# Linear-recurrence attention with a mixture of experts on one core: state products in four column tiles, squares kept in the keys' tile, the bounded norm's last two VectorE operations folded into one, and one state product given to ScalarE

## The chip, the core and the metric

The kernel runs on one core of a Trainium2 chip. The metric is the device time of one execution in microseconds, the median of several runs. The kernel before takes 1791.55 us (median of 3 runs, 1791.02 to 1792.45).

## What is computed

The reference has two parts. The first is a linear recurrence with complex decay, per batch (4) and head (8), over 768 steps with head dimension 48:

```python
mag = np.sqrt(a_re * a_re + a_im * a_im)
scale = np.minimum(mag, 0.999) / (mag + 1e-06)
a_re_n, a_im_n = (a_re * scale, a_im * scale)
for t in range(S):
    new_re = ar * S_re - ai * S_im          # ar, ai: step t's decay
    new_im = ar * S_im + ai * S_re
    kv = np.einsum('bhd,bhe->bhde', k[:, :, t], v[:, :, t])
    S_re, S_im = (new_re + kv, new_im)
    y[:, :, t] = np.einsum('bhd,bhde->bhe', q[:, :, t], S_re)
```

The second takes the outputs as 3072 tokens of 384 channels through 8 experts, `relu(x @ w1[e]) @ w2[e]` with 1024 hidden channels, weighted by a matrix that eight rounds of row and column normalisation make from `exp(x @ w_gate - max)`.

## The kernel before, in words

**Tokens and units.** The 3072 tokens are cut into 12 units of 256 steps (three for each batch entry), a unit into two chunks of 128 steps. Phase 1 (`phase1`, 0 to about 600 us) does the attention of unit i and at the same time experts 0 and 1 for unit i-1. Phases 2a and 2b do the normalisation and the experts 2 to 7, and touch nothing that the change touches.

**Elementwise part, `elem(i)` and `chain`.** For each unit VectorE and ScalarE turn the decays `z` into bounded decays (lines 386 to 400), form the running products of the decays over the chunk (`scan`, `cmul`, lines 283 to 288), and from their squared magnitude (lines 409 to 417) make keys divided by the running product (`kh`, line 420) and queries multiplied by it (written over `z`, line 422). In the bounded norm, line 396 gives `zz` as a Square on ScalarE, line 397 gives `x = min(-0.4995*y0, 1)` on VectorE, and line 398 gives `x = (zz + 0.75) * x` on VectorE. The first unit, `elem(0, scratch=True)`, goes in two halves with tiles of its own; units 1 to 11 go whole, on 128 x 768 elements a plane.

**Chunks, `mix(i)`.** For each chunk, 12 transfers (line 441) bring keys and queries into `ks` and `qs` (six `ks<-kh`, six `qs<-z`), with 112 used partitions: real parts in 0 to 47, imaginary parts in 64 to 111. TensorE transposes the keys (`keys`, line 460), multiplies keys with queries (`scores`, line 474), keys with values (`state`, line 469: the new state contribution `U`, 112 x 48 for each of 8 heads), and masked scores and old state with values and queries (`outs`, line 491). `outs` runs in four column tiles of the array, 32 columns each, one head in each tile. All these operands are four-byte floats; each such matmul is two instructions in the trace. VectorE then makes the next state: `tm = S0 + U` (line 517, left out where the state starts at zero), `sa = tm * rr` (line 524), two half products into `sb` (lines 526 and 527), and `S1 = sa + sb` (line 528). The last chunk of a batch entry makes no state, so 20 of the 24 chunks do this.

**Order.** TensorE's order is written out by hand: for unit i, 16 pieces of expert work of unit i-1 are sent, each of an `l2` (lines 158 to 160) and a first-layer product `ph` (lines 179 to 181); after piece n, from n = LEAD on (11 for unit 1, 10, 8, 6, then 4), one step of `mix` follows: keys, then scores and state, then nothing, then outs and the next chunk's keys. ScalarE copies each `ph` out twice (`hh`, `hf`, lines 185 and 186), VectorE subtracts them (`hl`, line 187). `ph` has two buffers. The orders of VectorE, ScalarE and the DMA queue of SyncE in this phase come from a scheduler that simulates the program, so an edit in one place can move instructions in others.

**Names.** `U` is a PSUM tile; `tm` and `sa` have one buffer each; `sq` (the squares of lines 390 and 409) has a tile of its own, `kh` another.

Of the kernel before, what the change touches and what calls it, by code (L numbers as in the profile page):

```python
# [6 lines left out]
F32 = mybir.dt.float32  # L7
F32R = mybir.dt.float32r
U8 = mybir.dt.uint8
AF = mybir.ActivationFunctionType  # L10
ALU = mybir.AluOpType
AX = mybir.AxisListType

H, D = 8, 48
# [8 lines left out]
SK = 112  # L23
# [20 lines left out]
def slot(h):  # L44
    return (h % 4) * 128 + (h // 4) * 80
# [9 lines left out]
class Net:  # L55
# [9 lines left out]
    def build(self):  # L65
        tc, nc = self.tc, self.nc
        DR = bass.MemoryType.DRAM
        PS = bass.MemoryType.PSUM
        with ExitStack() as ctx:
            dram = ctx.enter_context(tc.tile_pool(name="dram", bufs=1, space=DR))  # L70
            cst = ctx.enter_context(tc.tile_pool(name="cst", bufs=1))
            self.wp = ctx.enter_context(tc.tile_pool(name="wp", bufs=RING))
            self.psA = ctx.enter_context(tc.tile_pool(name="psA", bufs=2, space=PS))

            self.ones = cst.tile([128, 128], F32, name="ones")
            nc.vector.memset(self.ones, 1.0)
            warm = cst.tile([128, 1], F32, name="warm")
            nc.scalar.activation(warm, self.ones[:, 0:1], AF.Abs_reciprocal_sqrt)
            self.ident = cst.tile([128, 128], F32, name="ident")
            nc.sync.dma_start(self.ident, self.idn)  # L80
            self.nident = cst.tile([128, 128], F32R, name="nident")
            nc.scalar.activation(self.nident, self.ident, AF.Copy, scale=-1.0)
            self.mask = cst.tile([128, 4, CH], U8, name="mask")
            tri = cst.tile([128, CH], F32, name="tri")
            nc.sync.dma_start(tri, self.msk)
            for j in range(4):
                nc.vector.tensor_copy(self.mask[:, j, :], tri)
            self.bm05 = cst.tile([128, 1], F32, name="bm05")
            nc.vector.memset(self.bm05, -0.5)
            self.wgs = cst.tile([128, NCT, 2 * E], F32R, name="wgs")  # L90
            self.two = cst.tile([2 * E, E], F32, name="two")
            nc.vector.tensor_tensor(self.two, self.ident[:2 * E, :E], self.ident[:2 * E, E:2 * E], ALU.add)
            wgr = cst.tile([128, NCT, E], F32, name="wgr")
            nc.sync.dma_start(wgr, self.wg)
            nc.scalar.activation(self.wgs[:, :, :E], wgr, AF.Copy)
            nc.vector.tensor_tensor(self.wgs[:, :, E:], wgr, self.wgs[:, :, :E].bitcast(F32), ALU.subtract)
            self.P = cst.tile([128, self.ntt, E], F32, name="P")

            ns = self.N // SUB
            self.fl = cst.tile([128, ns * (NCT * NCH + 2) + 2], F32, name="fl")  # L100
            self.ok = cst.tile([128, 9], F32, name="ok")
            self.oki = cst.tile([1, 1], mybir.dt.int32, name="oki")
            self.wt = {}
            self.x_d = [dram.tile([128, NS, 2, NCT, 2, CH], F32, name=f"x_d{u}") for u in range(self.N // UN)]
            self.ye_d = [[dram.tile([128, C], F32, name=f"ye_d{u}_{i}") for i in range(self.ntt)] for u in range(2)]
            self.dram = dram

            with ExitStack() as c2, tc.manual_schedule(engines={mybir.EngineType.PE}):
                with ExitStack() as c1:
                    with ExitStack() as ca:  # L110
                        self.phase1(c1, ca)
                    self.phase2a(c2)
                self.phase2b(c2)
            flag = nc.values_load(self.oki[0:1, 0:1], min_val=0, max_val=1)
            with tc.If(flag < 1):
                with ExitStack() as c3:
                    self.general(c3)
# [257 lines left out]
    def chain(self, i, ns_, zt, qk, alloc):  # L375
        nc = self.nc
        V = nc.vector
        full = ns_.stop - ns_.start == NCH
        n0 = ns_.start
        G = NCT * (ns_.stop - n0)  # L380

        def cut(t):
            return t if full else t.rearrange("p a (c n) t -> p a c n t", n=NCH)[:, :, :, n0, :]

        z, qk = cut(zt[:, :, :, :CH]), cut(qk)
        fl, ns = self.fl, self.N // SUB
        base = 2 * ns + ns * NCT * NCH
        f0, f1 = (i, ns + i) if n0 == 0 else (base, base + 1)
        sq, x, y0, zz = alloc("sq"), alloc("x"), alloc("y0"), alloc("zz")
        nc.scalar.activation(sq, z, AF.Square, accum_out=fl[:, f0:f0 + 1])  # L390
        V.scalar_tensor_tensor(x, sq[:, 0], 1e-20, sq[:, 1], ALU.max, ALU.add)
        nc.scalar.activation(y0, x, AF.Abs_reciprocal_sqrt)
        nc.scalar.activation(zz, y0, AF.Square, accum_out=fl[:, f1:f1 + 1])
        V.tensor_tensor(x, x, zz, ALU.mult)
        V.scalar_tensor_tensor(y0, x, -3.0, y0, ALU.add, ALU.mult)
        nc.scalar.activation(zz, y0, AF.Square, bias=self.bm05, scale=-0.5e-6)
        V.tensor_scalar(x, y0, -0.4995, 1.0, ALU.mult, ALU.min)
        V.scalar_tensor_tensor(x, zz, 0.75, x, ALU.add, ALU.mult)
        for a in range(2):
            V.tensor_tensor(z[:, a], z[:, a], x, ALU.mult)  # L400
        if full or n0 == 0:
            self.scan(z, alloc)
        else:
            with self.tc.issue_after(self.last.ins):
                self.scan(z, alloc)
        for j in range(CH, ZW):
            nc.scalar.activation(cut(zt[:, :, :, j:j + 1]), z[:, :, :, CH - 1:CH], AF.Copy)
        sq, x, g0 = alloc("sq"), alloc("x"), alloc("g0")
        nc.scalar.activation(sq, z, AF.Square)
        V.scalar_tensor_tensor(x, sq[:, 0], 1e-26, sq[:, 1], ALU.max, ALU.add)  # L410
        o = 2 * ns + i * NCT * NCH + n0 * NCT
        nc.scalar.activation(fl[:, o:o + G], x[:, :, CH - 1], AF.Copy)
        nc.scalar.activation(g0, x, AF.Abs_reciprocal_sqrt)
        act = nc.scalar.activation(g0, g0, AF.Square)
        V.tensor_tensor(x, x, g0, ALU.mult)
        self.gl = V.scalar_tensor_tensor(g0, x, -2.0, g0, ALU.add, ALU.mult)
        V.scalar_tensor_tensor(x, g0, -1.0, qk[:, 1], ALU.mult, ALU.mult)
        kh = alloc("kh")
        for a in range(2):
            V.tensor_tensor(kh[:, a], x, z[:, a], ALU.mult)  # L420
        for a in range(2):
            dve = V.tensor_tensor(z[:, a], z[:, a], qk[:, 0], ALU.mult)
        if i == 0:
            self.acts.append(act)
            self.act0, self.dve0 = act, dve

    def mix(self, i):
        nc, tmp = self.nc, self.tmp
        vt = self.vt[i]
# [4 lines left out]
        for c in range(NCH):  # L434
# [29 lines left out]
            def state(g, c=c, U=U, kts=kts, lastc=lastc):  # L464
                if lastc:
                    return
                for j in range(4):
                    h = 4 * g + j
                    nc.tensor.matmul(U[:, h, :], kts[g][:, j, :], vt[:, c, slot(h):slot(h) + D], start=True, stop=True)  # L469

            def scores(g, i=i, c=c, ks=ks, qs=qs, sss=sss):
                sp = self.psS.tile([128, 4, CH], F32, tag="s", name=f"sp{i}_{c}_{g}")
# [37 lines left out]
            if not lastc:  # L510
                sh = [SK, 2, H // 2, D]
                Uv = U.rearrange("p (b q) d -> p b q d", b=2)
                if first:
                    tm = Uv
                else:
                    tm = tmp.tile([SK, H, D], F32, tag="tm", name=f"tm{i}_{c}", bufs=1).rearrange("p (b q) d -> p b q d", b=2)
                    nc.vector.tensor_tensor(tm, heads(S0), Uv, ALU.add)
                sa = tmp.tile([SK, H, D], F32, tag="sa", name=f"sa{i}_{c}", bufs=1).rearrange("p (b q) d -> p b q d", b=2)

                def bc(t):  # L520
                    return t.rearrange("p (b q) -> p b q", b=2).unsqueeze(3).broadcast_to([t.shape[0], 2, H // 2, D])

                sbv = self.sb.rearrange("p (b q) d -> p b q d", b=2)
                nc.vector.tensor_tensor(sa, tm, bc(rr), ALU.mult)
                h0, h1 = slice(0, D), slice(64, 64 + D)
                nc.vector.tensor_tensor(sbv[h0], tm[h1], bc(R[h1]), ALU.mult)
                nc.vector.tensor_tensor(sbv[h1], tm[h0], bc(rn[h0]), ALU.mult)
                nc.vector.tensor_tensor(heads(S1), sa, sbv, ALU.add)
                self.ist = 1 - self.ist
# [617 lines left out]
```

## Time and profile before

| what | value |
|---|---|
| median of 3 runs | 1791.55 us |
| the profiled execution's own time | 1792.06 us |
| its span, first to last instruction | 1790.3 us |
| mean granted TensorE clock | 0.994 |
| busy: TensorE matmuls, VectorE, ScalarE | 98%, 76%, 41% of the span |
| phase 1 (attention, experts 0 and 1) | 0 to about 600 us |

Times in the rows are microseconds; starts count from the first instruction of the profiled execution. PE is TensorE's matmul side, DVE VectorE, ACT ScalarE, SPq the DMA queue of SyncE. A row of a group names the line, the engine, the operation, the tile written and those read, the shapes and the count, then the busy time, the mean of one in nanoseconds and the idle time before. Matmuls are pipelined, so that a duration is longer than the distance to the next start; it is that distance that costs time. In a timeline a run of like instructions is one row, with its count behind the x, and in brackets the idle time before it and what ended that.

### The profile page before, as it was taken

To read this page: it belongs to the slowest core of one execution; us is meant where nothing else is said; L and a number is where in the kernel's file an instruction comes from. 1 tells how busy PE (TensorE), PEld (TensorE's weight loads), DVE (VectorE), ACT (ScalarE), POOL (GpSimd) and SP (SyncE) were. 2 spreads that over 40 slices of the span, in tenths; PEclk is the share of its full clock that TensorE was granted. 3 is DMA by queue.
4 is the path that set the end of the run, shared out by engine and by line. 5 is a ranking of instruction groups with operands and counts; after the bars stand their busy time and mean duration, and the time that the engine had idled before them with its cause. 6 is when DMAs were issued, how large, how long until landed. Compare 5 with 4: busy or idle time off the path is not lost.

```text
span 1790.3 us, 30678 instructions
## 1 busy us (share of the span) xinstructions
PE 1751.3 (98%) x12024; PEld 1725.8 (96%) x12024; DVE 1366.8 (76%) x3036; ACT 733.6 (41%) x1609; POOL 6.4 (0%) x15
## 2 busy tenths in 40 slices
PE   5889999999999999999999999999999999999998
PEld 3889999999999999999999999999999999999998
DVE  7898999999983678777777767687767777776754
ACT  7544544555543544443332424243433333332321
POOL 1000000000000000000000000000000000000000
PEclk9899999999999999999999999999999999999999
DMA  6333333334343420111111101232111111010100
GB/s 215 95 119 110 119 119 119 119 114 119 103 105 104 135 89 27 53 53 46 45 54 50 48 18 54 76 111 63 45 52 38 54 54 50 22 54 18 45 27 29
DMA packets 133689, 132.85 MB, mean 74 GB/s; under 512 B 10400, under 2 KB 125856, under 8 KB 133536
## 3 DMA queue, kind: packets, MB, share of 16 engines
q1 hardware_dynamic: 132736, 130.41, 24.3%
q8 instruction: 96, 1.57, 0.4%
q14 instruction: 57, 0.47, 0.1%
q10 hardware_dynamic: 800, 0.39, 0.1%
HBM read 88.22 MB, written 23.59 MB: 62 GB/s over the span
## 4 chain that ended last, share of the span: by engine, by line
PE 91%; DVE 6%; DMA 1%; ACT 1%; issue 1%; SPq 0%; ACTq 0%; DVEq 0%
PE po L800 11%; PE po L799 11%; PE po L798 11%; PE P L894 10%; PE P L896 10%; PE P L895 10%; PE po L158 4%; PE ph L180 4%; PE ph L181 4%; PE ph L179 3%; PE po L159 3%; PE po L160 3%; PE sp L474 2%; PE y L491 2%; PE U L469 1%; DMA wr<-in_w_dram 1%
## 5 line engine op out<-in xcount | busy, mean ns | idle before, releaser
L800 PE MATMUL po<-wc,hl 128*128 128x384 f32 x1152 | 385.0, 334 | 0.0
L799 PE MATMUL po<-wc,hh 128*128 128x384 f32 x1152 | 384.8, 334 | 0.0
L798 PE MATMUL po<-wc,hh 128*128 128x384 f32 x1152 | 384.8, 334 | 0.0
L914 ACT ACTIVATE hh<-c 128x384 fp32r<-128x384 f32 x384 | 201.6, 526 | 347.0 <-DVE c L904 347.0
L919 DVE SCALAR_TENSOR_TENSOR hl<-c,hh 128x384 fp32r<-128x384 f32 x384 | 212.5, 553 | 50.5 <-ACT hh L914 36.3
L909 ACT ACTIVATE s<-P 128x384 f32<-128x384 f32 x192 | 94.1, 490 | 317.8 <-PE P L896 317.8
L800 PEld LDWEIGHTS po<-wc,hl 128*128 128x128 f32 x1152 | 216.3, 188 | 0.3 <-DVE hl L919 0.2
L798 PEld LDWEIGHTS po<-wc,hh 128*128 128x128 f32 x1152 | 216.3, 188 | 0.0
L799 PEld LDWEIGHTS po<-wc,hh 128*128 128x128 f32 x1152 | 216.3, 188 | 0.0
L185 ACT ACTIVATE hh<-ph 128x256 fp32r<-128x256 f32 x192 | 73.5, 383 | 231.1 <-PE ph L181 230.6
L180 PE MATMUL ph<-xl,w 128*128 128x256 f32 x576 | 162.7, 282 | 3.3 <-DVE xl L531 3.3
L181 PE MATMUL ph<-xh,w 128*128 128x256 f32 x576 | 162.4, 282 | 0.0
L179 PE MATMUL ph<-xh,w 128*128 128x256 f32 x576 | 162.0, 281 | 0.0
L894 PE MATMUL P<-B,wa 128*128 128x384 f32 x480 | 160.8, 335 | 0.1
L896 PE MATMUL P<-B,wa 128*128 128x384 f32 x480 | 160.3, 334 | 0.0
L895 PE MATMUL P<-B,wa 128*128 128x384 f32 x480 | 160.3, 334 | 0.0
L158 PE MATMUL po<-w,hh 128*128 128x384 f32 x384 | 136.7, 356 | 0.0
L159 PE MATMUL po<-w,hh 128*128 128x384 f32 x384 | 129.6, 337 | 0.0
L160 PE MATMUL po<-w,hl 128*128 128x384 f32 x384 | 129.4, 337 | 0.0
L904 DVE TENSOR_TENSOR c<-P,u 128x384 f32<-128x384 f32 x192 | 106.7, 556 | 22.0 <-PE P L896 20.4
L187 DVE TENSOR_TENSOR hl<-hf,hh 128x256 fp32r<-128x256 f32 x192 | 81.0, 423 | 48.3 <-ACT hf L186 46.9
L180 PEld LDWEIGHTS ph<-xl,w 128*128 128x128 f32 x576 | 108.8, 189 | 4.0 <-DVE xl L531 4.0
(189 smaller groups left out, 3579.0 us busy)
## 6 DMA issues: line engine op xcount, KB each, us to landing
raw<-in_w_dram SPq DMA_DIRECT2D x96, 384.0 KB, 3.1
qs<-z SPq DMA_DIRECT2D x144, 64.5 KB, 2.6
qk<-in_aqk_dram SPq DMA_DIRECT2D x12, 768.0 KB, 4.7
ks<-kh SPq DMA_DIRECT2D x144, 64.0 KB, 2.6
ye_d<-yst SPq DMA_DIRECT2D x48, 192.0 KB, 1.9
y<-ye_d SPq DMA_DIRECT2D x48, 192.0 KB, 2.4
z<-in_aqk_dram SPq DMA_DIRECT2D x11, 768.0 KB, 6.6
B<-x_d SPq DMA_DIRECT2D x40, 192.0 KB, 3.4
```

What stands on the lines that cost most here:

```text
L158: nc.tensor.matmul(po[k], hh[:, s], w2h, start=f == 0, stop=False)
L179: nc.tensor.matmul(ph, w[:, 0, cs], xh[:, ct, :], start=(ct == 0), stop=False)
L180: nc.tensor.matmul(ph, w[:, 0, cs], xl[:, ct, :], start=False, stop=False)
L181: nc.tensor.matmul(ph, w[:, 1, cs], xh[:, ct, :], start=False, stop=(ct == NCT - 1))
L798: nc.tensor.matmul(po[k], hh[:, s], w2[:, 0, i], start=first, stop=False)
L799: nc.tensor.matmul(po[k], hh[:, s], w2[:, 1, i], start=False, stop=False)
L800: nc.tensor.matmul(po[k], hl[:, s], w2[:, 0, i], start=False, stop=last)
L894: nc.tensor.matmul(ps, t[:, 0, k], x[:, 0], start=first, stop=False)
L895: nc.tensor.matmul(ps, t[:, 0, k], x[:, 1], start=False, stop=False)
L896: nc.tensor.matmul(ps, t[:, 1, k], x[:, 0], start=False, stop=last)
L914: A.activation(hh, c, AF.Relu)
L919: V.scalar_tensor_tensor(hl, c, 0.0, hh.bitcast(F32), ALU.max, ALU.subtract)
```

## The change

There are four edits, all in phase 1.

- `state` (line 469): each head's matmul with 112 weight columns becomes four with 32, 32, 32 and 16 weight columns, at column tiles 0, 32, 64 and 96. Values and result are the same.
- `chain`, units 1 to 11: ScalarE computes `zz = -0.4995*zz - 0.75*0.4995` (Identity with a bias), and VectorE's lines 397 and 398 become one: `x = max(y0, -1/0.4995) * zz`. Unit 0 keeps the old form.
- `chain`: the second Square (line 409) is written into `kh`'s tile, which its keys overwrite later; the tile `sq` serves only the first Square.
- `mix`, units 2 to 11: `sa = tm * rr` becomes eight ScalarE activations, one for each head, with that head's column of `rr` as scale.

```diff
+            self.bw = cst.tile([128, 1], F32, name="bw")
+            nc.vector.memset(self.bw, -0.75 * 0.4995)
...
         nc.scalar.activation(zz, y0, AF.Square, bias=self.bm05, scale=-0.5e-6)
-        V.tensor_scalar(x, y0, -0.4995, 1.0, ALU.mult, ALU.min)
-        V.scalar_tensor_tensor(x, zz, 0.75, x, ALU.add, ALU.mult)
+        if i:
+            nc.scalar.activation(zz, zz, AF.Identity, bias=self.bw, scale=-0.4995)
+            V.scalar_tensor_tensor(x, y0, -1 / 0.4995, zz, ALU.max, ALU.mult)
+        else:
+            V.tensor_scalar(x, y0, -0.4995, 1.0, ALU.mult, ALU.min)
+            V.scalar_tensor_tensor(x, zz, 0.75, x, ALU.add, ALU.mult)
...
-        sq, x, g0 = alloc("sq"), alloc("x"), alloc("g0")
+        kh, x, g0 = alloc("kh"), alloc("x"), alloc("g0")
+        sq = kh
...
-        kh = alloc("kh")
...
-                    nc.tensor.matmul(U[:, h, :], kts[g][:, j, :], vt[:, c, slot(h):slot(h) + D], start=True, stop=True)
+                    for q in range(0, SK, 32):
+                        e = min(q + 32, SK)
+                        nc.tensor.matmul(U[q:e, h, :], kts[g][:, j, q:e], vt[:, c, slot(h):slot(h) + D], start=True, stop=True, tile_position=(0, q), skip_group_check=True)
...
-                nc.vector.tensor_tensor(sa, tm, bc(rr), ALU.mult)
+                if i < 2:
+                    nc.vector.tensor_tensor(sa, tm, bc(rr), ALU.mult)
+                else:
+                    for h in range(H):
+                        nc.scalar.activation(sa[:, h // 4, h % 4], tm[:, h // 4, h % 4], AF.Copy, scale=rr[:, h:h + 1])
```

TensorE's order is the same otherwise. The scheduler's orders move in many places; two matter here.

The first is VectorE at the end of unit 1's chain. This is its order before (`x_867`, `g_868` and `kh_877` belong to unit 1, `x_1434` and `zz_1436` to unit 2, `hl` to the experts of unit 0):

```order
L410 SCALAR_TENSOR_TENSOR x_867<-sq_866 128x768
L187 TENSOR_TENSOR hl_0_5_1006<-hf_0_5_1007,hh_0_5_1005 128x256
L391 SCALAR_TENSOR_TENSOR x_1434<-sq_1433 128x768
L187 TENSOR_TENSOR hl_0_6_1028<-hf_0_6_1029,hh_0_6_1027 128x256
L415 TENSOR_TENSOR x_867<-x_867,g_868 128x768
L187 TENSOR_TENSOR hl_0_7_1050<-hf_0_7_1051,hh_0_7_1049 128x256
L416 SCALAR_TENSOR_TENSOR g_868<-x_867,g_868 128x768
L187 TENSOR_TENSOR hl_0_0_1072<-hf_0_0_1073,hh_0_0_1071 128x256
L417 SCALAR_TENSOR_TENSOR x_867<-g_868,qk_769 128x768
L394 TENSOR_TENSOR x_1434<-x_1434,zz_1436 128x768
L187 TENSOR_TENSOR hl_0_1_1094<-hf_0_1_1095,hh_0_1_1093 128x256
L420 TENSOR_TENSOR kh_877<-x_867,z_768 128x768 x2
```

This is the same place in the changed kernel (unit 1 is `x_917`, `g_918`, `kh_916`; unit 2 is `x_1531`, `y_1532`, `zz_1533`):

```order
L417 SCALAR_TENSOR_TENSOR x_917<-kh_916 128x768
L189 TENSOR_TENSOR hl_0_3_1011<-hf_0_3_1012,hh_0_3_1010 128x256
L393 SCALAR_TENSOR_TENSOR x_1531<-sq_1530 128x768
L189 TENSOR_TENSOR hl_0_4_1033<-hf_0_4_1034,hh_0_4_1032 128x256
L422 TENSOR_TENSOR x_917<-x_917,g_918 128x768
L423 SCALAR_TENSOR_TENSOR g_918<-x_917,g_918 128x768
L189 TENSOR_TENSOR hl_0_5_1055<-hf_0_5_1056,hh_0_5_1054 128x256
L396 TENSOR_TENSOR x_1531<-x_1531,zz_1533 128x768
L424 SCALAR_TENSOR_TENSOR x_917<-g_918,qk_819 128x768
L189 TENSOR_TENSOR hl_0_6_1077<-hf_0_6_1078,hh_0_6_1076 128x256
L397 SCALAR_TENSOR_TENSOR y_1532<-x_1531,y_1532 128x768
L426 TENSOR_TENSOR kh_916<-x_917,z_818 128x768 x2
```

Unit 2's third norm operation (`y`) now stands ahead of unit 1's keys, and the expert subtractions stand two pieces later in the row. On ScalarE the Square of unit 2's decays, which the third of these rows reads, stood behind unit 1's `g` before, and now stands ahead of the copy of unit 0's last attention output, well before unit 1's second Square.

The second place is ScalarE in unit 6's second chunk. Before (`hh_5_0` and so on are expert 1's pieces for unit 5, `yst` finished expert outputs, `sq`, `fl` and `g` unit 7's chain, the second `sq` unit 8's):

```order
L185 ACTIVATE hh_5_0_4508<-ph_5_0_4498 128x256
L186 ACTIVATE hf_5_0_4510<-ph_5_0_4498 128x256
L185 ACTIVATE hh_5_1_4553<-ph_5_1_4543 128x256
L186 ACTIVATE hf_5_1_4555<-ph_5_1_4543 128x256
L163 ACTIVATE yst_5_0_4562<-po_5_0_4276 128x384
L409 ACTIVATE sq_4840<-z_4742 128x1536
L163 ACTIVATE yst_5_1_4568<-po_5_1_4280 128x384
L185 ACTIVATE hh_5_2_4581<-ph_5_2_4571 128x256
L186 ACTIVATE hf_5_2_4583<-ph_5_2_4571 128x256
L412 ACTIVATE fl<-x_4841 128x6
L413 ACTIVATE g_4842<-x_4841 128x768
L390 ACTIVATE sq_5431,fl<-z_5425 128x1536
```

The same place in the changed kernel (`zz` belongs to unit 8's norm, `sa` to this chunk's state):

```order
L187 ACTIVATE hh_5_0_4817<-ph_5_0_4807 128x256
L188 ACTIVATE hf_5_0_4819<-ph_5_0_4807 128x256
L398 ACTIVATE zz_5835<-y_5834,bm_81 128x768
L400 ACTIVATE zz_5835<-zz_5835,bw 128x768
L187 ACTIVATE hh_5_1_4886<-ph_5_1_4876 128x256
L188 ACTIVATE hf_5_1_4888<-ph_5_1_4876 128x256
L165 ACTIVATE yst_5_0_4895<-po_5_0_4554 128x384
L536 ACTIVATE sa_1_4954<-tm_1_4952,rr_194 112x48 x2
L165 ACTIVATE yst_5_1_4901<-po_5_1_4558 128x384
L536 ACTIVATE sa_1_4954<-tm_1_4952,rr_194 112x48 x6
L187 ACTIVATE hh_5_2_4914<-ph_5_2_4904 128x256
L188 ACTIVATE hf_5_2_4916<-ph_5_2_4904 128x256
```

The squares have moved to earlier places, and the eight state products now stand in front of the copies of the next piece's `ph`.

## The prediction

> **What bounds the kernel now.** I read the page's busy shares and its chain first, then the engines by stretch, then the rows around one state product.
>
> ```profile
> PE 1751.3 (98%) x12024; PEld 1725.8 (96%) x12024; DVE 1366.8 (76%) x3036; ACT 733.6 (41%) x1609; POOL 6.4 (0%) x15
> ...
> PE 91%; DVE 6%; DMA 1%; ACT 1%; issue 1%; SPq 0%; ACTq 0%; DVEq 0%
> ```
>
> TensorE is busy 98% of the span and is 91% of the chain that ended last. By stretch (busy microseconds of TensorE's matmuls, its weight loads, VectorE, ScalarE and GpSimd, the granted clock, DMA):
>
> ```profile
> 150.00:300.00 150.00, 148.85 (x1439) 144.72 (x1438) 138.11 (x342) 70.26 (x186) 0.00 (x0) 1.00 0.40 120
> 300.00:450.00 150.00, 150.00 (x1440) 146.78 (x1439) 138.64 (x316) 78.94 (x198) 0.00 (x0) 1.00 0.40 120
> 450.00:600.00 150.00, 150.00 (x1390) 146.92 (x1390) 104.63 (x254) 64.22 (x176) 0.00 (x0) 1.00 0.39 114
> ```
>
> From 150 to 600 us TensorE waits for about 1 us in all: what it saves there shortens the run, as long as VectorE (138.64 of 150) and ScalarE (78.94 of 150) keep up. Before 150 it has gaps, and there another engine decides. Two that the change can reach are these (the bracket is the idle time and who ended it):
>
> ```profile
> 98.88 1.73 PE L460 MATMUL ktp<-ident,ks 112*128 112x112 f32 x8 [3.70 <-DMA ks<-kh]
> ...
> 103.88 2.02 PE L474 MATMUL sp<-qs,ks 112*128 112x128 f32 x16 [0.46 <-DMA qs<-z]
> ```
>
> At unit 1 TensorE waits 3.70 us for keys and 0.46 for queries: here unit 1's chain on VectorE sets the time, through the transfers.
>
> **The state product.** First its group, then the place where it runs in unit 6, and then a stretch of `outs`, the kernel's existing column tiles.
>
> ```profile
> L469 PE MATMUL U<-v,kt 128*112 128x48 f32 x320 | 33.7, 258 | 0.0
> ```
>
> ```profile
> 328.21 0.28 PE L181 MATMUL ph<-xh,w 128*128 128x256 f32 x1
> 328.32 1.95 PE L474 MATMUL sp<-qs,ks 112*128 112x128 f32 x16
> 330.11 1.68 PE L469 MATMUL U<-v,kt 128*112 128x48 f32 x16
> 331.62 0.42 PE L158 MATMUL po<-w,hh 128*128 128x384 f32 x1
> 331.88 0.34 PE L159 MATMUL po<-w,hh 128*128 128x384 f32 x1
> 332.05 0.34 PE L160 MATMUL po<-w,hl 128*128 128x384 f32 x1
> ```
>
> ```profile
> 300.61 0.28 PE L181 MATMUL ph<-xh,w 128*128 128x256 f32 x1
> 300.81 0.43 PE L491 MATMUL y<-sc,v 128*32 128x128 f32 x8
> 301.06 0.41 PE L491 MATMUL y<-qs,st 112*32 112x128 f32 x8
> 301.28 0.41 PE L491 MATMUL y<-sc,v 128*32 128x128 f32 x8
> ...
> 302.38 0.41 PE L491 MATMUL y<-qs,st 112*32 112x128 f32 x8
> 302.72 0.44 PE L158 MATMUL po<-w,hh 128*128 128x384 f32 x1
> 303.00 0.34 PE L159 MATMUL po<-w,hh 128*128 128x384 f32 x1
> ```
>
> Read distances between starts. `scores`: 16 instructions from 328.32 to 330.11, so 0.112 us each, for 128 weight columns and 128 streamed. `U`: 16 from 330.11 to 331.62, and the next row lasts 0.42 instead of 0.34, so (1.51 + 0.08) / 16 = 0.099 each. It streams only 48 columns, which at the pace of `scores` would be 0.112 x 48/128 = 0.042; 112 weight columns at that pace are 0.098. So **U is held by its weight loads**. `outs`: a row of x8 (four tiles, two instructions each) starts every 0.22 us, 0.11 for a set of four, as much as one `scores` instruction alone. Four tiles load and stream side by side at no extra time.
>
> New U: 8 heads x 2 instructions = 16 sets of four, each streaming 48 columns with 32 weight columns (0.028 at the same pace, and hidden, as in `outs`). The ends are 0.042 a set, if the stream sets the pace, and the 0.112 of `outs`, if the set's pace doesn't fall with the columns: 0.67 to 1.79 us. I take 0.045, near the stream, since in both neighbours the longer of stream and load set the pace: 0.72.
>
> Going into column tiles and out again costs something in `outs`. In: 300.61 to 300.81 is 0.20 where 328.21 to 328.32 is 0.11, and the first x8 takes 0.25 instead of 0.22, together 0.12. Out: the last x8 would end at 302.60, `po` starts at 302.72, and the next follows 0.28 later instead of 0.17 (331.88 to 332.05): 0.23. So from U's start to the second `po` instruction it is 0.12 + 0.72 + 0.23 + 0.17 = 1.24 us, against 331.88 - 330.11 = 1.77 now: **0.53 less for each chunk**. x320 is 20 chunks; unit 0's two lie where TensorE waits anyway and count nothing. 18 x 0.53 = 9.5 us.
>
> The Trainium skill, "TensorEngine Tiling (Array Packing)", Instruction Overhead, speaks against part of this: it gives each matmul some 60 cycles of overhead, so that fewer than 60 streamed columns gain nothing more. By it a set would cost as 60 columns do, an estimate of 0.053, and the sum would be 2 us smaller. The rows have no matmul of fewer than 128 columns that is not held by its loads, so they can't say.
>
> **VectorE and ScalarE.**
>
> ```profile
> L524 DVE TENSOR_TENSOR sa<-tm,rr 112x384 f32<-112x384 f32 x16 | 8.9, 554 | 0.1
> L397 DVE TENSOR_SCALAR x<-y 128x768 f32<-128x768 f32 (+1 forms) x13 | 6.8, 527 | 0.1
> ```
>
> ```profile
> L396 ACT ACTIVATE zz<-y,bm 128x768 f32<-128x768 f32 (+1 forms) x13 | 11.6, 889 | 4.5 <-DVE y L395 4.5
> L503 ACT ACTIVATE rr<-qs 48x8 f32<-48x8 f32 x20 | 4.3, 214 | 0.2
> ```
>
> VectorE loses 16 state products (20 chunks less the four of units 0 and 1) of 0.554 and 11 norm operations of about 0.55, 15 us in all, between 50 and 570 us. ScalarE gains 11 x 0.89 = 10 us, and 16 x 8 activations of 48 elements: nearest is 0.214 for 8 elements; the other end is 0.38 for the 256 of an `hf` copy (its row stands under rival A). I take 0.22, so 1.8 us a chunk and 28 us in all, up to 49. Neither is TensorE's time after 150 us. VectorE's relief of 15 us is more than TensorE's gain of 9.5, so it doesn't become the bound. The new waits: S1's sum waits for ScalarE's products, covered by the scan operations that stand between; nothing of TensorE needs S1 before the next chunk's `outs`, several pieces of expert work later. Behind the products on ScalarE stand `hh` and `hf`, for which the `ph` buffers wait: that is rival A.
>
> Squares in the keys' tile: they now wait until the preceding unit's keys have left it.
>
> ```profile
> 323.69 3.80 SPq L441 DMA_DIRECT2D ks<-kh  x6
> ```
>
> ```profile
> 346.58 1.50 ACT L409 ACTIVATE sq<-z 128x1536 f32<-128x1536 f32 x1
> ```
>
> Unit 6's last key transfers go out from 323.69 to 327.5; unit 7's Square runs at 346.58. Some 16 us cover the wait, so it costs nothing.
>
> **The start, unit 1's chain.** Here VectorE is the bound, and its order moves.
>
> ```profile
> 85.93 0.96 DVE L391 SCALAR_TENSOR_TENSOR x<-sq 128x768 f32<-128x768 f32 x1 [2.15 <-ACT sq L390]
> ...
> 87.21 0.96 DVE L415 TENSOR_TENSOR x<-x,g 128x768 f32<-128x768 f32 x1
> 88.08 0.42 DVE L187 TENSOR_TENSOR hl<-hf,hh 128x256 fp32r<-128x256 f32 x1
> ...
> 92.03 1.82 DVE L420 TENSOR_TENSOR kh<-x,z 128x768 f32<-128x768 f32 x2
> ```
>
> The norm operation saves 0.5 (line 397's mean); the Identity that replaces it (0.89) follows the Square (0.89) while VectorE does `sa`, two `sb` and S1's sum (four of 0.55), so it is hidden. At 85.93 VectorE had waited 2.15 us for unit 2's Square, which ScalarE now does much earlier. Next late is then unit 1's `g`: ScalarE has no Square of 1.4 to 1.5 us (1.47 under rival A) in between, so line 415 comes about 1.4 earlier. Unit 2's `y` now stands ahead of the keys: 0.87 (87.21 to 88.08) back. Keys: 0.5 + 1.4 - 0.87 = 1.0 earlier. Queries, behind that `y` either way: 1.9. Against it, `hl` stands later, which delays TensorE's expert work by some 2 us, but that is inside the 3.70. Bounds: a gain of no more than 3.70 + 0.46 = 4.2, and a loss of up to 1.8 if both ScalarE operations (2 x 0.89) came uncovered. I take 1.8, since the last gate at 103.88 is the queries.
>
> **Sum.** 9.5 + 1.8 = 11.3 us. Against the profiled execution (1792.06, of which the span is 1790.3) that is 1780.8; it was 0.5 above the median of the runs, so against 1791.55 it is **1780.3**.
>
> **Rivals.**
>
> A. *ScalarE holds TensorE.* The margin was thin in places. Unit 5's second chunk, ScalarE and then TensorE:
>
> ```profile
> 305.86 1.47 ACT L390 ACTIVATE sq<-z 128x1536 f32<-128x1536 f32 x1
> 307.32 0.36 ACT L185 ACTIVATE hh<-ph 128x256 fp32r<-128x256 f32 x1
> 307.59 0.38 ACT L186 ACTIVATE hf<-ph 128x256 f32<-128x256 f32 x1
> ```
>
> ```profile
> 308.09 0.31 PE L179 MATMUL ph<-xh,w 128*128 128x256 f32 x1
> ```
>
> The copy ended at 307.97 and the `ph` that reuses the buffer began at 308.09: 0.12 to spare. Another 1.8 us in that place would stop TensorE for 1.7. In all ten units from 2 on that is 17 us, and the run 1797; in three of them it is 5 us, and 1785. Against it: the products stand behind U, and the second `ph` after U is followed by `outs` before the next reuse, which adds 1.8 us (300.81 to 302.60) to the margin; and the Squares have moved away. Chance 0.16, mostly the partial form.
>
> B. *Instructions come too slowly* (slower). A set of four in `outs` takes 0.11 us, 0.028 an instruction. The rows don't say whether the stream or the supply of instructions sets this, since both would give it. If supply, U's 64 instructions take 1.79 us, a chunk 0.12 + 1.79 + 0.23 + 0.17 = 2.31, 0.54 more than now: 18 x 0.54 = +9.7, with the start 1799.5. It decides from 0.09 a set up. For it: 64 instructions in 0.72 us would be 2.5 times the densest stretch of this trace. Against it: one untiled `scores` instruction takes the same 0.112, so the stream explains `outs` alone. Chance 0.10. The Trainium skill, "TensorE: Matmul & The Clock Gate", section "Wait — 56ns, not 53.3ns?", puts a floor of about 25 ns between matmul starts, however small; over 64 that would be an estimate of 1.6 us.
>
> C. *Column tiles load their weights one after another.* U keeps 1.57 us and pays 0.35 for going in and out, less the 0.08 that it pays now: +0.24 x 18 = +4.3, with the start 1794. `outs` can't show it, as its four loads of 32 columns in turn would also be 0.11. Chance 0.07.
>
> **Chances.** Forecast 0.67 (1776.5 to 1784), A 0.16, B 0.10, C 0.07. The lower end is U at 0.042 (0.9 us) and the start at its bound (2.4 us); the upper end goes to 1789, through most of A, and leaves out B, C and the worst of A, not quite 2 in 10. Within 0.2% is 3.6 us, about what a measurement of this kernel can tell from no change. Faster: the forecast and most of A, 0.81. Slower: B, the worst of A and a little of C, 0.12. The rest, mostly C, 0.07.
>
> **What would show it.** U's run should last 0.7 to 0.9 us with `po` 0.1 late behind it. TensorE should still wait for nothing from 150 to 600, and less than 3.70 at unit 1. Busy VectorE should fall by 15 us, busy ScalarE rise by 38. A `ph` waiting for `hf` means A; a U of 1.5 us or more means B or C.

## The result, and the profile after

The changed kernel takes **1806.97 us** (median of 4 runs, 1802.88 to 1809.52), the kernel before, run beside it, 1791.28 us: a ratio of 1.0086 (95% interval 1.0074 to 1.0098). It is 15.7 us slower, where 11.3 us less had been forecast, and lies outside the range given. The profiled execution took 1809.52 us, the longest of the four.

First the busy line and the chain that ended last, from the page of the changed kernel:

```profile
PE 1754.6 (97%) x12984; PEld 1721.6 (95%) x12984; DVE 1355.9 (75%) x3010; ACT 768.0 (42%) x1748; POOL 6.4 (0%) x15
...
PE 84%; DVE 6%; DMA 4%; ACT 3%; issue 2%; SPq 2%; ACTq 0%; DVEq 0%
```

TensorE was 91% of the chain and is 84%; transfers, ScalarE and SyncE's queue have come in. The same three stretches as before (TensorE's matmuls, its weight loads, VectorE, ScalarE, GpSimd, granted clock, DMA):

```profile
150.00:300.00 150.00, 145.70 (x1703) 140.11 (x1702) 134.76 (x327) 83.28 (x234) 0.00 (x0) 0.98 0.39 118
300.00:450.00 150.00, 141.16 (x1551) 136.22 (x1550) 130.90 (x299) 82.90 (x228) 0.00 (x0) 0.97 0.38 112
450.00:600.00 150.00, 148.42 (x1678) 143.96 (x1677) 94.27 (x230) 70.28 (x212) 0.00 (x0) 0.99 0.34 105
```

TensorE now waits 14.7 of these 450 us, and the granted clock, 1.00 before, is 0.97 to 0.99. VectorE is less busy than before in all three. Over the whole run its busy time fell by 10.9 us and ScalarE's rose by 34.4, where 15 and 38 had been forecast.

The state product itself did what was forecast. TensorE in unit 6, the second chunk:

```profile
331.91 1.95 PE L482 MATMUL sp<-qs,ks 112*128 112x128 f32 x16
333.79 0.88 PE L477 MATMUL U<-v,kt 128*32 128x48 f32 x64
334.60 0.44 PE L160 MATMUL po<-w,hh 128*128 128x384 f32 x1
334.88 0.34 PE L161 MATMUL po<-w,hh 128*128 128x384 f32 x1
```

From U's start to the second `po` it is 1.09 us, and U starts 0.09 later behind `scores` (1.88 instead of 1.79): 1.18 where 1.24 was forecast and 1.77 stood before.

What is new is a wait of ScalarE. Rows of the waits (us in total, how often, the longest):

```profile
ACT sq L392 <- DMA z<-in_aqk_dram: 38.5, 10, 6.9
DVE hl L189 <- ACT hf L188: 62.4, 47, 4.0
```

The first of these did not exist before; the second was 46.9. Line 392 is the first Square of a unit's norm, which reads the freshly loaded decays `z`. ScalarE at such a place, unit 10's load (the bracket is the idle time and what ended it):

```profile
417.21 0.38 ACT L188 ACTIVATE hf<-ph 128x256 f32<-128x256 f32 x1
422.84 1.48 ACT L392 ACTIVATE sq<-z 128x1536 f32<-128x1536 f32 x1 [5.25 <-DMA z<-in_aqk_dram]
424.23 0.19 ACT L392 ACTIVATION_READ_ACCUMULATOR sq<-z 128x1 f32 x1
424.32 0.36 ACT L187 ACTIVATE hh<-ph 128x256 fp32r<-128x256 f32 x1
424.59 0.37 ACT L188 ACTIVATE hf<-ph 128x256 f32<-128x256 f32 x1
424.85 0.36 ACT L558 ACTIVATE ls<-lp 16x256 f32<-16x256 f32 x1
425.12 0.83 ACT L165 ACTIVATE yst<-po 128x384 f32<-128x384 f32 x2
425.86 1.47 ACT L416 ACTIVATE kh<-z 128x1536 f32<-128x1536 f32 x1
```

The first Square of unit 10 stands ahead of the second Square of unit 9 (line 416), and everything behind it waits with it: the copies of `ph`, the copy `ls` that the router needs, and unit 9's own chain. TensorE meanwhile:

```profile
421.40 0.28 PE L182 MATMUL ph<-xl,w 128*128 128x256 f32 x1
421.52 0.28 PE L183 MATMUL ph<-xh,w 128*128 128x256 f32 x1
425.26 1.01 PE L562 MATMUL lt<-two,ls 16*128 16x8 f32 x4 [3.47 <-ACT ls L558]
...
428.93 0.41 PE L181 MATMUL ph<-xh,w 128*128 128x256 f32 x1
429.15 0.41 PE L182 MATMUL ph<-xl,w 128*128 128x256 f32 x1
```

It stops for 3.47 us, and after the stop a `ph` instruction takes 0.21 us from start to start instead of 0.12. The stretches around it show why (columns as above):

```profile
421.00:424.00 3.00, 0.80 (x7) 0.59 (x5) 0.83 (x3) 1.16 (x1) 0.00 (x0) 1.00 0.15 41
424.00:428.00 4.00, 2.74 (x10) 2.71 (x11) 1.07 (x2) 3.92 (x11) 0.00 (x0) 0.55 0.26 98
428.00:432.00 4.00, 4.00 (x20) 4.00 (x19) 1.95 (x4) 1.55 (x5) 0.00 (x0) 0.60 0.00 0
```

The granted clock, as a mean over these stretches, fell to 0.55 and 0.60: the stop is paid a second time. The Trainium skill, "TensorE: Matmul & The Clock Gate", section "HAM oscillation — how this bites in real kernels", says that TensorE goes to half its clock when it idles for more than about 3.4 us; this stop agrees. But in this trace a stop of 2.29 us is also followed by half pace, for the 3.4 us in which the granted clock is 0.50 (the row behind it, with the columns of the stretches):

```profile
379.99 0.57 PE L181 MATMUL ph<-xh,w 128*128 128x256 f32 x1 [2.29 <-ACT hf L188]
...
380.99 0.41 PE L182 MATMUL ph<-xl,w 128*128 128x256 f32 x1
381.21 0.41 PE L183 MATMUL ph<-xh,w 128*128 128x256 f32 x1
```

```profile
380.04:383.44 3.40, 3.32 (x14) 3.02 (x15) 2.33 (x4) 3.36 (x10) 0.00 (x0) 0.50 0.00 0
```

Before, the same Square (line 390) had no wait. Unit 10's load went out on SyncE's queue at 419.97 and had landed, by the trace, at 426.17; on ScalarE the second Square of unit 9 came first, and that of unit 10 behind it:

```profile
419.97 0.39 SPq L308 DMA_DIRECT2D z<-in_aqk_dram  x1
```

```profile
431.21 1.49 ACT L409 ACTIVATE sq<-z 128x1536 f32<-128x1536 f32 x1
...
435.07 1.47 ACT L390 ACTIVATE sq<-z 128x1536 f32<-128x1536 f32 x1
```

The second loss is in the phases that the change doesn't touch. The last `y` of the attention and the last `po` of the second phase, before and then after (instructions, shortest, median and longest in nanoseconds, first and last start):

```profile
L491 PE MATMUL y<-sc,v x768: 270/273/298, 50.9 to 582.2; 128*32 128x128 f32 x192
L800 PE MATMUL po<-wc,hl x1152: 334/334/444, 640.0 to 1784.0; 128*128 128x384 f32 x192
```

```profile
L499 PE MATMUL y<-sc,v x768: 270/273/423, 51.8 to 595.0; 128*32 128x128 f32 x192
L812 PE MATMUL po<-wc,hl x1152: 334/334/440, 652.8 to 1800.8; 128*128 128x384 f32 x192
```

From one to the other it was 1201.8 us and is 1205.8, for the same 6988 matmuls. So 12.8 us were lost before the last `y`, and 4.0 behind it.

### The profile page after: what moved, and what is told of

It is laid out like the page before. It is cut to its first block, busy times and chain, and to the rows that moved or that the text cites. A ratio compares the mean times of both kernels' runs of the same rounds, so it can differ in the third digit from the quotient of the medians.

```text
span 1807.7 us, 32788 instructions
## 1 busy us (share of the span) xinstructions
PE 1754.6 (97%) x12984; PEld 1721.6 (95%) x12984; DVE 1355.9 (75%) x3010; ACT 768.0 (42%) x1748; POOL 6.4 (0%) x15
## 4 chain that ended last, share of the span: by engine, by line
PE 84%; DVE 6%; DMA 4%; ACT 3%; issue 2%; SPq 2%; ACTq 0%; DVEq 0%
PE po L810 11%; PE po L812 11%; PE po L811 11%; PE P L907 10%; PE P L908 10%; PE P L906 10%; PE po L160 3%; PE ph L182 3%; PE ph L183 3%; PE ph L181 3%; PE po L162 3%; PE po L161 3%; DMA z<-in_aqk_dram 2%; PE sp L482 2%; SPq L447 1%
## 5 line engine op out<-in xcount | busy, mean ns | idle before, releaser
L916 DVE TENSOR_TENSOR c<-P,u 128x384 f32<-128x384 f32 x192 | 106.8, 556 | 22.8 <-PE P L908 21.1
L181 PEld LDWEIGHTS ph<-xh,w 128*128 128x128 f32 x576 | 109.7, 190 | 4.6 <-ACT hf L188 3.7
```

What stands on the lines that cost most here:

```text
L181: nc.tensor.matmul(ph, w[:, 0, cs], xh[:, ct, :], start=(ct == 0), stop=False)
```

## The experiments

For each kernel the table gives the median (or the one time), the start of the last `y`, TensorE's idle time up to it (the gaps between one matmul's end and the next one's start, added up from the trace), its work (what is left from the start of its first matmul, at 10.9 to 12.5 us, to the last `y`), and the time from the last `y` to the end of the last matmul. The kernel before, run with each group, gave medians of 1791.28 to 1792.29.

| kernel | us | last y | idle | worked | second phase |
|---|---|---|---|---|---|
| before | 1791.3 | 582.5 | 21.1 | 550.1 | 1201.9 |
| after | 1807.0 | 595.2 | 33.7 | 549.2 | 1206.0 |
| u_only | 1785.7 | 576.9 | 25.2 | 539.8 | 1201.9 |
| sq_only | 1800.2 | 590.9 | 24.7 | 554.1 | 1201.9 |
| no_sq | 1792.1 | 577.2 | 25.4 | 539.6 | 1205.9 |
| held | 1792.0 | 576.3 | 26.4 | 537.8 | 1205.9 |
| u_pad | 1790.2 | 576.8 | 25.0 | 539.3 | 1206.0 |
| held_al | 1788.0 | 578.3 | 25.9 | 540.4 | 1201.9 |
| after_al | 1806.2 | 597.6 | 37.3 | 548.2 | 1201.9 |
| u_padh (one run) | 1795.5 | 575.9 | 26.6 | 537.1 | 1212.1 |
| u_padw (one run) | 1797.4 | 576.2 | 25.1 | 538.8 | 1213.5 |
| u_pad64 (one run) | 1787.7 | 576.2 | 24.8 | 539.3 | 1203.7 |
| u_al64 | 1785.9 | 576.3 | 24.6 | 540.3 | 1201.9 |
| u_sa | 1786.2 | 575.6 | 23.8 | 539.8 | 1201.9 |
| u_norm_al | 1786.4 | 577.4 | 25.0 | 540.2 | 1201.9 |
| u_lite (one run) | 1784.3 | 574.5 | 22.4 | 539.8 | 1202.1 |
| u_sq | 1793.1 | 583.0 | 27.6 | 544.6 | 1202.0 |
| no_sa | 1815.1 | 602.6 | 42.5 | 549.2 | 1205.9 |
| no_norm | 1818.8 | 605.1 | 42.8 | 549.9 | 1205.9 |

### Which edit

*The theory: with the squares in the keys' tile nothing forces a unit's first Square behind the second Square of the unit before, the scheduler puts it ahead, and ScalarE blocks on a load that lands later. The rivals: the work moved to ScalarE is at fault, or a faster TensorE is no use.*

**u_only**: before with the new `state` loop alone.

```diff
-                    nc.tensor.matmul(U[:, h, :], kts[g][:, j, :], ...)
+                    for q in range(0, SK, 32):
...
+                        nc.tensor.matmul(U[q:e, h, :], kts[g][:, j, q:e], ..., tile_position=(0, q), ...)
```

> Before with the column tiles alone. If the gain on TensorE is real and only hidden by another edit: 18 chunks x 0.53 = 9.5 us less, 1780 to 1784, and TensorE waits for nothing from 150 to 600 us. If another engine or the transfers would be the bound as soon as TensorE is faster (rival): the waits come with this edit alone, and the time is 1789 us or more.

1785.7 us, ratio 0.9968 (0.9958 to 0.9979). TensorE's work up to the last `y` falls by 10.3 us where 9.5 were forecast, but its idle time rises by 4.1, nearly all of it before 250 us, and its first matmul starts 0.7 later. So neither text was quite right: the gain is real and a part of it turns into waits.

**sq_only**: before with the squares in the keys' tile alone.

```diff
-        sq, x, g0 = alloc("sq"), alloc("x"), alloc("g0")
+        kh, x, g0 = alloc("kh"), alloc("x"), alloc("g0")
+        sq = kh
...
-        kh = alloc("kh")
```

> Before with the squares in the keys' tile alone. Theory: the second Square of a unit and the first Square of the next no longer share a tile, so the next unit's first Square is put ahead in ScalarE's order and stops it there until that unit's load lands; ScalarE waits 20 us or more for the load, TensorE waits behind it, and the run is slower, 1795 to 1805. Rival (the state products on ScalarE are at fault, and this edit costs nothing): within 2 us of before, and no wait of ScalarE for the load.

1800.2 us, ratio 1.0047 (1.0030 to 1.0063): 8.5 us slower, by this edit alone. Its waits have the row that the theory asks for:

```profile
ACT sq L390 <- DMA z<-in_aqk_dram: 27.6, 10, 5.1
```

**no_sq**: after without that edit, its diff the reverse of the last one.

> After with the second Square back in the first Square's tile, the other three edits kept. Theory: the wait of ScalarE for the load goes, the gain of the column tiles comes through, 1778 to 1784. Rival (the products or the norm operation on ScalarE are at fault): 1797 or more, with TensorE waiting for hf or for S1's products.

1792.1 us, ratio 1.0004 (0.9994 to 1.0014). ScalarE no longer waits for the load, and the last `y` is as early as in u_only, so the rival falls; but the total was forecast 8 to 14 us lower. The missing part is in the second phase (4 us) and in the waits that u_only showed (4 us).

**held**: after with all four edits, but the order that the old tile enforced written into the code.

```diff
-        nc.scalar.activation(sq, z, AF.Square, accum_out=fl[:, f0:f0 + 1])
+        with ExitStack() as st:
+            if i > 1:
+                st.enter_context(self.tc.issue_after(self.sq2.ins))
+            nc.scalar.activation(sq, z, AF.Square, accum_out=fl[:, f0:f0 + 1])
...
-        nc.scalar.activation(sq, z, AF.Square)
+        self.sq2 = nc.scalar.activation(sq, z, AF.Square)
```

> After with all four edits, but from unit 2 on the first Square of a unit is issued behind the second Square of the unit before it. Theory (only the order on ScalarE does the damage): 1779 to 1786, and ScalarE's wait for the load falls from 38.5 us to under 10. Rival (the tile itself does it, because the second Square now waits for the key transfers): 1797 or more, as after.

1792.0 us, ratio 1.0005 (0.9996 to 1.0015), and the last `y` at 576.3 instead of 595.2. **The order of the first Square, with what the scheduler moves along with it, made 15 us of the median.** (The 18.9 us between the two profiled executions say more than that: the one of after was its slowest run, the one of held its fastest.) ScalarE's wait for the load falls to this:

```profile
ACT sq L395 <- DMA z<-in_aqk_dram: 1.5, 1, 1.5
```

And ScalarE at the same place as above:

```profile
413.07 1.49 ACT L419 ACTIVATE kh<-z 128x1536 f32<-128x1536 f32 x1 [1.28 <-DVE z L290]
414.46 1.47 ACT L395 ACTIVATE sq<-z 128x1536 f32<-128x1536 f32 x1
```

The first Square now follows the second and finds its data there. The second Square in the keys' tile keeps its new wait for the key transfers, and that costs nothing that shows, as the prediction had it. The total misses the expectation for the same two reasons as that of no_sq.

### The second phase: where the tiles lie

The new constant `bw` is a tile of one column in the pool that is allocated first. In the built program it takes 32 bytes in each partition, and the weights, `hh`, `hl` and the transformed inputs `B` and `T` behind it, which all started at multiples of 64 bytes, start 32 bytes further up.

**u_pad**: u_only and an unused tile at that place. TensorE and ScalarE have the order of u_only.

```diff
             nc.vector.memset(self.bm05, -0.5)
+            pad = cst.tile([128, 1], F32, name="pad")
+            nc.vector.memset(pad, 0.0)
```

> Before with the column tiles, and a tile of one unused column (32 bytes in each partition) where the change has its new constant: every weight tile, hh, hl and the transformed inputs then lie 32 bytes further up, as in after; the order on TensorE and ScalarE is that of u_only. Theory (the place of the operands in memory costs 4 us in the second phase): from the last y to the end 1205.9 us instead of 1201.9, and 1789 to 1791 in all. Rival (the second phase became slower through the edits themselves): 1201.9, and 1785 to 1787.

1790.2 us, 4.5 more than u_only; the last `y` is at the same time to 0.1 us, and the second phase takes 1206.0. The two rows of u_pad:

```profile
L495 PE MATMUL y<-sc,v x768: 270/273/423, 51.9 to 576.6; 128*32 128x128 f32 x192
L804 PE MATMUL po<-wc,hl x1152: 334/334/443, 634.4 to 1782.5; 128*128 128x384 f32 x192
```

The median row doesn't show it: the distances between starts, 173 or 174 ns almost throughout before, spread from 170 to 185, and the mean over the phase is 0.3% up.

**held_al** and **after_al**: held and after with the constant in the unused rest of the old one's 32 bytes, so that nothing moves.

```diff
-            self.bm05 = cst.tile([128, 1], F32, name="bm05")
...
-            self.bw = cst.tile([128, 1], F32, name="bw")
...
+            bias = cst.tile([128, 2], F32, name="bias")
+            self.bm05, self.bw = bias[:, 0:1], bias[:, 1:2]
```

> held, with the new constant in the unused rest of the 32 bytes that the old one has, so that no other tile moves. Theory: the second phase takes 1201.9 us again, the first one stays as in held (last y at 576), 1786 to 1789 in all. Rival (the place in memory doesn't matter): 1205.9, and 1791 to 1793.

> After with all four edits and its order, but with the new constant in the old one's 32 bytes, so that nothing else moves. Theory (the costs add up: the order of the first Square some 15 us, the place in memory 4): second phase 1201.9, 1800 to 1804 in all, ScalarE's wait for the load still 25 us or more. If the place in memory is all that went wrong: 1786 or less.

held_al: 1788.0 us, ratio 0.9979 (0.9970 to 0.9989), second phase 1201.9, as expected. after_al: second phase 1201.9 and ScalarE's wait 40.9 us, as expected; but 1806.2 us in all, above the 1800 to 1804, since its first phase came out 2.4 us longer in the profiled execution than that of after. That is not another order: in the two traces every engine has the same operations in the same order. The four runs of each kernel lie 5 to 7 us apart (1802.73 to 1808.11, and 1802.88 to 1809.52), so their medians can hardly show 4 us, and the place in memory is shown by the second phase alone.

**u_padh**, **u_padw**, **u_pad64**, **u_al64**: u_only with unused bytes elsewhere. u_padh moves `hh`, `hl`, `B` and `T` by 32; u_padw the weights by 32 and these by 64; u_pad64 all by 64; u_al64 the attention's own tiles by 32. The first of these diffs, the others are alike:

```diff
             self.wp = ctx.enter_context(tc.tile_pool(name="wp", bufs=RING))
+            pad = ctx.enter_context(tc.tile_pool(name="pad", bufs=1)).tile([128, 1], F32, name="pad")
```

> Before with the column tiles, and the unused 32 bytes behind the ring of the weights: the weights stay where they are in before, and hh, hl and the transformed inputs of the second phase lie 32 bytes further up. If it is the weights' place that costs the 4 us, the second phase takes 1201.9 us; if it is that of hh, hl and the transformed inputs, 1205.9; if both share in it, something between.

> Before with the column tiles; unused bytes put the weights 32 bytes up and hh, hl and the transformed inputs 64 bytes up, so that only the weights start off a multiple of 64 bytes. If what counts is that the two lie alike (both on, or both off, a multiple of 64): second phase 1207 us or more, as bad as with the activations off alone (1212.1). If the activations' own place counts: 1201.9. If each counts by itself and the weights' shift helps once the activations are off: below 1201.9 is not to be had, so 1202 to 1204.

> Before with the column tiles, and 64 unused bytes where u_pad has 32: weights and activations all start at multiples of 64 bytes again. If the multiple of 64 counts: second phase 1201.9 us. If any shift against the tiles at the other end of the memory costs: 1205 or more.

> Before with the column tiles, and 32 unused bytes at the other end of the memory, so that the first phase's z, kh, keys, scores, states and values start at multiples of 64 bytes (in before they start 32 past one); the order is that of u_only. If TensorE loses there in the first phase what it loses in u_pad in the second (0.34% of the some 130 us of its work on these tiles), it is 0.4 us faster than u_only: no difference that can be measured, 1784 to 1787. If the other engines lose from it too, last y comes 1 us or more earlier than 576.9.

1212.1, 1213.5, 1203.7 and 1201.9 us of second phase. Moving one side by 32 against the other costs 10 to 12 us, moving both 4.1; that the two lie alike matters more than where each lies, which u_padh's expectation didn't foresee. But both up by 64 still costs 1.9, so a multiple of 64 is not the whole rule, and which one it is stays open. In the first phase no such loss shows in any of them, and the attention's tiles (u_al64, ratio 0.9967, as u_only) don't mind their place.

### The other two edits, and the waits that the gain turned into

**u_sa** is u_only with the products on ScalarE, **u_norm_al** u_only with the folded norm (constant placed as in held_al); their diffs are the parts of the change.

> Before with the column tiles and the state products on ScalarE. If the products are harmless and bring nothing, as no_sq against u_only lets expect: last y at 576 to 578, 1784 to 1787 in all. If they hold TensorE (rival A of the prediction): TensorE waits for hf or for y's operands in every unit, last y at 579 or later, 1788 or more.

> Before with the column tiles and the folded norm operation, its constant placed as in held_al. If the fold shortens VectorE's chain where that decides (the first units): last y 0.5 to 2 us earlier than in u_only (575 to 576.5), 1783 to 1786. If the Identity on ScalarE lies bare in that chain: last y 1 to 4 us later, 1787 to 1790.

1786.2 us (0.9970, 0.9959 to 0.9981) and 1786.4 us (0.9971, 0.9961 to 0.9982): by themselves both are harmless and bring nothing, and TensorE waits for no `hf` in either. Rival A, with the products as the cause, is gone.

**u_lite**: u_only without the two products into `sb` in units 1 to 3, so that the state which later chunks read lacks that part.

```diff
-                nc.vector.tensor_tensor(sbv[h0], tm[h1], bc(R[h1]), ALU.mult)
-                nc.vector.tensor_tensor(sbv[h1], tm[h0], bc(rn[h0]), ALU.mult)
+                if i not in (1, 2, 3):
+                    nc.vector.tensor_tensor(sbv[h0], tm[h1], bc(R[h1]), ALU.mult)
+                    nc.vector.tensor_tensor(sbv[h1], tm[h0], bc(rn[h0]), ALU.mult)
```

> Before with the column tiles, and without the two products of the turned state (sb) in units 1 to 3, so the state that later chunks read lacks that part: 2 x 0.56 us less for VectorE in each of six chunks. If VectorE's work in the first units is what TensorE now waits for, its idle time from 100 to 600 us falls from 8 us to 5 or less and the last y comes at 574 or earlier. If the chain through the transfers or ScalarE holds it, idle time and last y (576.9) stay within 1 us.

TensorE's idle time behind 100 us falls from 8.3 to 6.2 us (behind 110 us from 8.3 to 5.4) and the last `y` comes 2.5 us earlier: in the direction expected, though neither mark (5 and 574) was reached. VectorE's work in the first units is a good part of what TensorE waits for there. The waits have this form, in u_only at unit 1:

```profile
118.61 0.43 PE L493 MATMUL y<-sc,v 128*32 128x128 f32 x8 [1.71 <-DVE sc L479]
```

The masked scores come late from VectorE; before, TensorE did not wait there. The products moved to ScalarE can't mend this, as they begin with unit 2, and the fold didn't.

### How long the block lasts

**u_sq**: u_only with the squares in the keys' tile. **no_sa** and **no_norm**: after without the products, and without the fold (its constant kept, so that the tiles lie as in after).

> Before with the column tiles and the squares in the keys' tile. Theory: the order of the first Square costs about what it does alone (8.5 us), so 1792 to 1796, and the rest of the 15 us comes from the products and the Identity that stand on ScalarE behind the blocked Square. Rival (a faster TensorE has less cover for the block): 1798 to 1802.

> After with the state products back on VectorE; tiles lie as in after. If the products behind the blocked Square make up the second half of the 15 us: 1798 to 1801. If the Identity does: 1805 to 1808, as after.

> After with the two norm operations on VectorE as before, the new constant still there, so that the tiles lie as in after. If the products make up the second half: 1805 to 1808, as after. If the Identity does: 1798 to 1801.

u_sq: 1793.1 us, 7.4 more than u_only, about what the edit costs alone. So the faster TensorE isn't what doubles it in after. no_sa and no_norm: 1815.1 us (ratio 1.0127, 1.0110 to 1.0144) and 1818.8 us (1.0152, 1.0136 to 1.0169). **Both expectations fall**: taking either of the two edits out makes it worse than after. ScalarE's wait for the load differs little between the four (38.5 us in after; here u_sq, no_sa, no_norm):

```profile
ACT sq L390 <- DMA z<-in_aqk_dram: 35.0, 10, 7.5
```

```profile
ACT sq L392 <- DMA z<-in_aqk_dram: 38.6, 10, 5.5
```

```profile
ACT sq L392 <- DMA z<-in_aqk_dram: 40.8, 10, 6.9
```

What differs is who stands behind. The router's `lt` waits for the copy `ls` for nothing in u_sq, where `ls` runs ahead of the block (409.58 against a Square at 415.75), and else, from 100 to 600 us, after first, then no_sa, then no_norm:

```profile
PE lt L562 <- ACT ls L558: 4.3, 2, 3.5
```

```profile
PE lt L558 <- ACT ls L554: 5.3, 1, 5.3
```

```profile
PE lt L558 <- ACT ls L554: 8.1, 2, 5.1
```

Each edit gives the scheduler another order, and what it happens to put behind the blocked Square is a part of the price. These rows are a part of the difference only; the rest was not taken apart, so why the block costs 7 to 9 us in sq_only and u_sq and 15 or more with the other edits stays open.

## Why the prediction was wrong

**The state product: right.** 0.53 us for each chunk was forecast; 0.59 was measured, and TensorE's work fell by 10.3 us in u_only against 9.5. Rivals B and C are gone. (C was also priced too low: 0.12 + 1.57 + 0.23 + 0.17 is 2.09, so 0.32 more for each chunk and not 0.24. And the lower end of the range is 1777.0 by its own terms, not 1776.5. Neither changes the forecast.) The 64 instructions start within 0.68 us, 0.043 for a set of four. So two figures of the Trainium skill that the prediction weighed against it are not borne out in the way it used them: the floor of 25 ns between starts ("TensorE: Matmul & The Clock Gate", section "Wait — 56ns, not 53.3ns?"), by which it would be 1.6 us, and the overhead of some 60 cycles ("TensorEngine Tiling (Array Packing)", Instruction Overhead), by which a set would take 0.053 by the prediction's estimate. On one and the same column tile two instructions start 0.043 us apart, so a floor of 25 ns for each tile is not tested.

**"Neither is TensorE's time after 150 us ... VectorE's relief of 15 us is more than TensorE's gain of 9.5, so it doesn't become the bound": wrong in size.** A sum over 500 us was set against a sum. A part of TensorE's gain turned into waits, most of them at single places before 250 us, where little of the relief lies: 4.1 of the 10.3 us in u_only, which has no relief, and 4.4 in no_sq, which has it.

**"Squares in the keys' tile ... Some 16 us cover the wait, so it costs nothing": the step that failed.** This term was put at nothing and cost 15 us. The sentence weighed only the wait that the shared tile adds, and was right about that (held). What the old tile did besides was not asked: `sq` served both Squares and so kept a unit's first one behind the last unit's second. With that dependence gone the scheduler put the first Square ahead, where its load on the chip lands later; presumably its simulation has the load earlier, which was not tried. The prediction even saw the Square move, and counted it as a gain ("which ScalarE now does much earlier", "the Squares have moved away"), without looking when `z` lands. The trace of before had the answer: load at 426.17, Square at 435.07, a margin of 9 us that the new order spent. Price: 15 us of the median. Of the 18.9 us between the profiled executions of after and held, 7.3 are more idle time (33.7 against 26.4) and 11.4 slower work (549.2 against 537.8). The slower work is the lower clock: up to the last `y` the granted clock stands at half for 41.0 us in after and for 17.1 in held, and 23.9 us more at half are 12 us of work lost. So ScalarE did hold TensorE, as rival A said, but through a load and not through the products; A had counted the moved Squares in its disfavour.

**The new constant: not costed at all.** 32 bytes of memory moved the experts' operands: 4.1 us.

**The start: right in size, wrong in its reason.** Unit 1's `scores` came at 102.40 us instead of 103.88, 1.5 earlier against the 1.8 forecast. But in u_only, which has no edit in the chain, they came at 102.17, and in sq_only at 104.50. The moved norm did not bring it, so the size was luck; what did bring it is open.

**The products and the fold:** by themselves at nothing (u_sa, u_norm_al), as costed; their relief of VectorE was worth nothing either.

From kernel to kernel on the medians: before to u_only -5.7 (columns), to held_al +2.3 (products, fold and tile together), to held +4.0 (place), to after +15.0 (order). Such steps add up by their making and prove nothing more; by another way, from held_al to after_al, the order is 18.2, and from there the place 0.7, with the spread of those runs in both. The best version found is u_only, 1785.7 us; adding the products, the fold or another placement to it gave no more.

## What to carry to other kernels

A buffer that two operations share is also an order between them. Before giving one of them another buffer, look what the scheduler may now put first, and when the data of that operation lands: on an engine that works its queue in order, one early instruction stops all behind it. And keep the addresses of the tiles that the hottest loop reads when a small constant is added; put it into padding that is there already.

## What the hardware showed that was not expected

- Matmuls of four-byte floats took 0.3% longer with weights and activations both 32 bytes up, and 0.8 to 1.0% longer (10.2 and 11.6 of 1201.9 us, one run each) with one of them 32 bytes off against the other. The rule behind it is open.
- Stops of TensorE well below 3 us can halve its pace, and not at once. In no_sa, after a stop of 1.75 us, `po` instructions still start 0.17 us apart, and a microsecond later `ph` comes every 0.21 us instead of 0.12. The two rows behind them are stretches, with the granted clock third from the end: it is 0.50 for 3.4 us and then 1.00.

```profile
206.11 0.44 PE L160 MATMUL po<-w,hh 128*128 128x384 f32 x1 [1.75 <-ACT yst L165]
206.39 0.33 PE L161 MATMUL po<-w,hh 128*128 128x384 f32 x1
206.56 0.34 PE L162 MATMUL po<-w,hl 128*128 128x384 f32 x1
...
207.45 0.41 PE L181 MATMUL ph<-xh,w 128*128 128x256 f32 x1
207.67 0.42 PE L182 MATMUL ph<-xl,w 128*128 128x256 f32 x1
```

```profile
207.03:210.44 3.41, 3.41 (x32) 3.12 (x34) 1.98 (x4) 1.99 (x3) 0.00 (x0) 0.50 0.29 105
210.45:212.00 1.55, 1.55 (x30) 1.35 (x23) 1.53 (x3) 0.91 (x3) 0.00 (x0) 1.00 0.00 0
```

- What a stop does hangs also on where it lies in a grid. In the traces of all 19 kernels the granted clock is 0.50 or 1.00 up to the last `y`, and changes only at whole multiples of 3.41 us from its first change. A stretch of this grid at full clock with more than 1.95 us of stops was always followed by one at half clock, one with less than 1.1 us never; between the two it came out either way. The stop of 1.75 us above lies whole in one such stretch, from 203.62 to 207.03.

- Sets of four column tiles with 48 streamed columns start every 0.043 us, 11 ns for each instruction.
